# Staging VectorE and ScalarE work a step apart in a fused attention and two-MLP kernel

## The chip, the cores and the metric

The kernel runs on one core of a Trainium2 chip. The metric is device time in microseconds (us) of one execution: the median of several runs. TensorE (PE in the profile, its weight loads PEld) multiplies; VectorE (DVE) and ScalarE (ACT) do the elementwise work; SyncE (SP) starts nearly all DMAs. Each engine takes its instructions strictly in the order in which the program lists them for it.

## The reference

```python
# attention, per batch of 2:  S = 3008 tokens, 256 features, z has 64
scores = (1/S) * z @ z.T
x = u * (np.maximum(scores, 0)**2 @ v)          # 6016 x 256 over both batches
# first MLP, d_ff = 2048, scalars s and b
h = x @ w_in;  r = np.maximum(h, 0);  x = (s * (r*r) + b) @ w_out
# second MLP
h = x @ w_in2; x = (h / (1 + np.exp(-1.702*h))) @ w_out2
```

All inputs and the output are fp32.

## The kernel before

Every fp32 operand is split into a high part (a ScalarE copy that rounds to the matmul's type) and a low part (a VectorE subtract), and a product is three matmuls: high by high, high by low, low by high. The work is one list of 672 steps, built in advance:

- **Attention**, steps 0 to 287. A `Fresh` step makes a 128 x 512 block of scores; a `Turned` step uses the transpose of an earlier block, parked in HBM and fetched again (`park`, `fetch`). The second batch begins at step 144. `load_z` and `load_v` bring a column's inputs; `split_z` and `split_v` split them.
- **First MLP, plain part**, steps 288 to 319: two chunks of 512 tokens (m = 0 and 1), 16 `Mlp` steps each, one per slice of 128 of the 2048 hidden features. `up` is six matmuls into a PSUM bank, `between` is the elementwise work, `down` six matmuls into the two accumulators of the chunk. Beside it run `add_w` (adds the second weights over all 16 slices into `total`, from which `add_rows` gets the bias b times the sum, `shift`), and `sum_w` (sums of first weights that the later steps need).
- **First MLP, quads**, steps 320 to 479: five pairs of chunks (p = 1 to 5; the last pair has 448 tokens a chunk). A `Quad` does two slices for two chunks in four steps with seven products instead of eight, which costs extra adds on VectorE (`join`, line 691) and copies out of PSUM on ScalarE (`save`, line 681).
- **Second MLP**, steps 480 to 671: six pairs of the same kind, with the sigmoid gate.

The end of the kernel body is the order of everything. At position i of the main loop the program lists, in this order: step k = i + 5's `up` and `between`, what was put off until k (`due`, sorted by a rank), the side jobs planned for i (`todo`, filled by `when`), and then step i's `down`. So a step has five positions between its `up` and its `down`. Side jobs are the loads, the splits, the decoding of the weights (`decode_w`, five parts for each of 32 half-slices in each layer, on VectorE and ScalarE, whose result goes to HBM and comes back with `fetch_w`), and the preparation of the next pair (`gate`, `parts_of`, `split_part`). Below, a position is counted from the first `Mlp` step (288): "position 13" is i = 301.

Tiles come from small pools: five `w` tiles for raw, decoded and fetched weights, four `zu` tiles, 14 `big` tiles, four `a` and six each of `hi` and `lo` tiles, four PSUM banks `ps` and two pairs of accumulators.

When a chunk of the first MLP is done, `post` scales it and adds the bias: one ScalarE instruction for each of two halves (line 535), and stores the result to HBM.

Of the kernel before, what the change touches and what calls it, by code (L numbers as in the profile page):

```python
# [7 lines left out]
F32 = mybir.dt.float32  # L8
# [7 lines left out]
def attention_mlp_mlp_kernel(  # L16
# [24 lines left out]
    nc = tc.nc  # L41
# [32 lines left out]
    def ring_tile(name):  # L74
        return ring.tile([P, CH], F32R, tag="ring", name=name)
# [156 lines left out]
    def decode_w(layer, j, k, part):  # L232

        raw = staged["w", layer, j, k]
        low, high = raw[:, 0, :], raw[:, 1, :]
        if part == 0:
            pw = staged["pw", layer, j, k] = bits.tile([P, CH // 2], U32, tag="pw", name="pw")
            nc.vector.tensor_scalar(pw, high, 20, 0x7FF, ALU.logical_shift_right, ALU.bitwise_and)  # L240
        elif part == 1:
            pw = staged["pw", layer, j, k]
            nc.scalar.activation(out=pw, in_=pw, func=AF.Relu, scale=float(2**23), bias=rebias[:, 0:1])
            mt = staged["mt", layer, j, k] = bits.tile([P, CH // 2], U32, tag="mt", name="mt")
            nc.vector.tensor_scalar(mt, high, 0xFFFFF, 0x100000, ALU.bitwise_and, ALU.bitwise_or)
        elif part == 2:
            mt = staged["mt", layer, j, k]
            fr = staged["fr", layer, j, k] = bits.tile([P, CH // 2], F32, tag="fr", name="fr")
            nc.vector.scalar_tensor_tensor(fr, low, 2.0**-32, mt, ALU.mult, ALU.add)
        elif part == 3:  # L250
            pw = staged["pw", layer, j, k]
            nc.vector.scalar_tensor_tensor(pw, high, 0x80000000, pw, ALU.bitwise_and, ALU.bitwise_or)
        else:
            pw, fr = staged["pw", layer, j, k], staged["fr", layer, j, k]
            if k == 0:
                staged["wf", layer, j] = mid_tile(f"wf_{layer}_{j}")
            half = staged["wf", layer, j].rearrange("p (k n) -> p k n", k=2)[:, k, :]
            nc.vector.scalar_tensor_tensor(half, fr, 2.0**-20, pw.bitcast(F32), ALU.mult, ALU.mult)
            if k == 1:
                wf[layer, j] = hbm.tile([P, CH], F32, tag=f"wf_{layer}_{j}", name=f"wfh_{layer}_{j}")  # L260
                nc.sync.dma_start(out=wf[layer, j], in_=staged.pop(("wf", layer, j)))

    def fetch_w(layer, j):
        staged["wf", layer, j] = mid_tile(f"wb_{layer}_{j}")
        nc.sync.dma_start(out=staged["wf", layer, j], in_=wf[layer, j])

    def sum_w(layer, i):

        a1, a2 = [staged["wf", layer, 2 * i + n][:, : 2 * P].rearrange("p (k f) -> p k f", k=2) for n in range(2)]
        t = ew.tile([P, CH], F32, tag="a", name="ws", bufs=4)  # L270
        s1, s2, s3, s4 = [t[:, n * P : (n + 1) * P] for n in range(4)]
        nc.vector.tensor_tensor(out=s1, in0=a2[:, 0], in1=a2[:, 1], op=ALU.add)
        nc.vector.tensor_tensor(out=s2, in0=s1, in1=a1[:, 0], op=ALU.subtract)
        nc.vector.tensor_tensor(out=s3, in0=a1[:, 0], in1=a2[:, 0], op=ALU.subtract)
        nc.vector.tensor_tensor(out=s4, in0=a1[:, 1], in1=s2, op=ALU.subtract)
        both = sums[layer, i] = room[i // 2][:, i % 2]
        nc.scalar.copy(out=both[:, 0], in_=t)
        nc.vector.tensor_tensor(out=both[:, 1], in0=t, in1=both[:, 0], op=ALU.subtract)

    def add_w(j):  # L280

# [27 lines left out]
    def split_w(layer, j):  # L309
        src2 = staged["wf", layer, j].rearrange("p (k n) -> p k n", k=2)  # L310
        for k, ws in enumerate((wi, wo)):
            w = ring_tile(f"w_{layer}_{j}_{k}").rearrange("p (h n) -> p h n", h=2)
            nc.scalar.copy(out=w[:, 0, :], in_=src2[:, k, :])
            nc.vector.tensor_tensor(out=w[:, 1, :], in0=src2[:, k, :], in1=w[:, 0, :], op=ALU.subtract)
            ws[layer, j] = w
        wi[layer, j] = wi[layer, j].rearrange("p h (k f) -> p h k f", k=2)

# [151 lines left out]
    class Mlp:  # L469
# [15 lines left out]
                )  # L485

        def between(self):
            n = self.n
            a = ew.tile([P, CH], F32, tag="a", name="a", bufs=4)
            hi = self.hi = ew.tile([P, CH], F32R, tag="hi", name="hi", bufs=6)  # L490
            lo = self.lo = ew.tile([P, CH], F32R, tag="lo", name="lo", bufs=6)
            nc.scalar.activation(out=a[:, :n], in_=self.p[:, :n], func=AF.Relu)
            nc.scalar.activation(out=a[:, :n], in_=a[:, :n], func=AF.Square)
            nc.scalar.copy(out=hi[:, :n], in_=a[:, :n])
            nc.vector.tensor_tensor(out=lo[:, :n], in0=a[:, :n], in1=hi[:, :n], op=ALU.subtract)

        def down(self):
            j = self.j
            if j == 0:
                self.acc[:] = acc_pair(self.acc.pop(), "accm")  # L500
            add_hidden(self.layer, j, self.hi, self.lo, self.n, self.acc, j == 0, j == NF - 1)
            if j == NF - 1:
                for d in range(2):
                    post(self.layer, self.m, d, self.acc)

    def add_hidden(layer, j, hi, lo, n, acc, first, last, hold=False):
        w = wo[layer, j]
# [15 lines left out]
        for i, d in order:  # L523
            if hold and d == 1:
                held.append((add, i, d))
            else:
                add(i, d)

    def post(layer, m, h, acc):
        start, n = tokens(m)  # L530
        if layer == 0:
            if h == 0:
                staged["y"] = big_tile(f"y_{m}").rearrange("p (d n) -> p d n", d=2)
            y = staged["y"]
            nc.scalar.activation(
                out=y[:, h, :n], in_=acc[h][:, :n], func=AF.Identity, scale=sb[:, 0:1], bias=shift[:, h : h + 1]
            )
            if h == 1:
                store_rows(1, m, y)
            return  # L540
# [65 lines left out]
        )[k]  # L606
        nc.vector.tensor_tensor(out=x[to], in0=x[first], in1=x[second], op=ALU.subtract)

    def split_part(layer, p, k):
        n = tokens(2 * p)[1]  # L610
        src = staged["parts", layer, p][TERMS[k]]
        to = big_tile(f"op_{layer}_{p}_{k}", F32R).rearrange("p (h n) -> p h n", h=2)
        xs[layer, p, TERMS[k]] = to
        nc.scalar.copy(out=to[:, 0, :n], in_=src)
        nc.vector.tensor_tensor(out=to[:, 1, :n], in0=src, in1=to[:, 0, :n], op=ALU.subtract)

    banks = []

# [210 lines left out]
    for bb in range(B):  # L829
        for c in range(NCH):  # L830
            first = at["f", bb, 0, c, 0]
            v0 = min(at["f", bb, c, c, 0], at.get(("t", bb, 0, c, 0), len(steps)))
            if (bb, c) == (0, 0):
                sz = -20
                when(-40, load_z, bb, c)
                when(-18, load_v, bb, c)
            else:
                sz = first - LAG - 10 if (bb, c) != (0, 1) else -12
                ahead = 14 if (bb, c) in ((1, 0), (1, 1)) else 0
                when(max(sz - 8 - ahead, -39 if bb == 0 and c < 2 else -LAG), load_z, bb, c)  # L840
                when(max(v0 - LAG - 16 - ahead, -17), load_v, bb, c)
            for i in range(3):
# [14 lines left out]
    slots = ([turns[i * len(turns) // (10 * NF)] for i in range(10 * NF)], range(at["m", 1, 2], len(steps)))  # L857
    for layer in range(2):
        n = 0
        for j in range(NF):  # L860
            for k in range(2):
                when(slots[layer][n - 6] if n > 5 else slots[layer][0] - (4 if layer else 14) + n, load_w, layer, j, k)
                for part in range(5):
                    when(slots[layer][n], decode_w, layer, j, k, part)
                    n += 1
        for j in range(NF):
            if layer == 0:
                free = [2 + 5 * (i + 1) for i in range(LASTC)]
                i = next((i for i in range(LASTC) if 2 * j + 2 <= free[i]), LASTC)
                p = ends[i] + 2 * (j - (free[i - 1] // 2 if i else 0))  # L870
            else:
                p = at["q", 0, NP - 1, j // 2] + 4 + 2 * (j % 2)
                if j % 2:
                    when(p + 1, sum_w, layer, j // 2)
            when(p - (5 if layer else 8), fetch_w, layer, j)
            when(p, split_w, layer, j)
    start = at["m", 0, 0]
    for n, i in enumerate((0, 1, 2, 3, 6, 7, 4, 5)):
        use = start + 4 + 3 * n // 2
        for j in (2 * i, 2 * i + 1):  # L880
            when(use - 2, fetch_w, 0, j)
            when(use, add_w, j)
        if i < 6:
            when(use, sum_w, 0, i)
        else:
            for j in (2 * i, 2 * i + 1):
                when(start + 21 + i, fetch_w, 0, j)
            when(start + 23 + i, sum_w, 0, i)
    when(start + 15, add_rows)
    for i in (0, 0, 12, 28):  # L890
        when(start + i, settle)
    for m in range(2):
# [6 lines left out]
    for layer in range(2):  # L899
        for p in range(1 - layer, NP):  # L900
            first = at["q", layer, p, 0] - LAG
            for x in range(4):
# [79 lines left out]
```

## Time and profile before

| | |
|---|---|
| Median of 3 runs | 1492.48 us (1492.07 to 1494.46) |
| Profiled execution: its time, and its span from first to last instruction | 1493.18 us, 1491.3 us |
| TensorE busy | 1446.3 us, 97% of the span |
| VectorE busy | 1163.5 us, 78% |
| ScalarE busy | 1117.8 us, 75% |
| Mean granted TensorE clock | 0.991 |

The profile is of one execution. Busy time of the TensorE includes matmuls that ran at a lower clock. Idle time of an engine matters only where it ends up on the path that sets the end.

### The profile page before, as it was taken

How to read it: one execution, taken by the hardware profiler on the slowest of the kernel's cores; microseconds unless marked ns; L12 is line 12 of the kernel's file. 1: busy time of each engine (PE TensorE's matmuls, PEld its weight loads, DVE VectorE, ACT ScalarE, POOL GpSimd, SP SyncE). 2: the span in 40 equal slices, each digit the busy share in tenths (PEclk: the TensorE clock that was granted, in tenths of full speed). 3: DMA queues.
4: the chain of work that ended last, by engine and by line, in shares of the span. 5: the costliest groups of instructions: out<-in, count | busy, mean ns of one | idle time of the engine just before them, and what ended most of it. 6: DMA issues, size and time to landing. Idle time of an engine off the chain costs nothing.

```text
span 1491.3 us, 19079 instructions
## 1 busy us (share of the span) xinstructions
PE 1446.3 (97%) x6404; PEld 1201.4 (81%) x6404; DVE 1163.5 (78%) x2202; ACT 1117.8 (75%) x2068; POOL 0.3 (0%) x6
## 2 busy tenths in 40 slices
PE   8999999999999779999999999999999999999998
PEld 6888888888888667888878788877888888888896
DVE  7898988898897745877777676888878787787875
ACT  8888777988797666788878787886756666666664
POOL 0000000000000000000000000000000000000000
PEclk9999999999999989999999999999999999999999
DMA  5686784776795713213141312220020202020001
GB/s 130 180 213 192 213 226 106 186 214 187 196 233 128 236 43 101 62 44 91 37 106 43 99 43 92 74 73 27 1 57 1 57 1 57 1 45 9 16 14 25
DMA packets 191458, 143.86 MB, mean 96 GB/s; under 512 B 131712, under 2 KB 155776, under 8 KB 188800
## 3 DMA queue, kind: packets, MB, share of 16 engines
q1 hardware_dynamic: 188160, 142.03, 36.1%
q8 instruction: 50, 0.82, 0.2%
q10 hardware_dynamic: 3200, 0.62, 0.2%
q14 instruction: 48, 0.39, 0.1%
HBM read 87.69 MB, written 54.92 MB: 96 GB/s over the span
## 4 chain that ended last, share of the span: by engine, by line
PE 83%; ACT 7%; DVE 6%; DMA 1%; issue 1%; SPq 0%; ACTq 0%; DVEq 0%
PE accq L515 28%; PE ps_d L636 7%; PE ps_b L636 7%; PE ps_c L636 7%; PE acc L325 4%; PE acc L324 4%; PE acc L329 4%; PE tac L324 3%; PE tac L325 3%; PE ps_a L636 3%; PE tac L329 3%; PE ps_h L483 2%; PE ps_s L347 2%; PE ps_s L348 2%; PE accm L515 2%; DVE lo L730 1%
## 5 line engine op out<-in xcount | busy, mean ns | idle before, releaser
L515 PE MATMUL accq<-hi,w 128*128 128x512 f32 (+1 forms) x1408 | 375.0, 385 | 0.1
L729 ACT CAST hi<-a 128x512 fp32r<-128x512 f32 (+1 forms) x352 | 210.6, 609 | 181.5 <-DVE a L718 133.7
L515 PEld LDWEIGHTS accq<-hi,w 128*128 128x128 f32 x1408 | 264.2, 188 | 49.9 <-ACT hi L729 0.7
L730 DVE TENSOR_TENSOR lo<-a,hi 128x512 fp32r<-128x512 f32 (+1 forms) x352 | 233.1, 675 | 63.5 <-ACT hi L729 56.6
L515 PE MATMUL accq<-lo,w 128*128 128x512 f32 (+1 forms) x704 | 218.0, 385 | 0.0
L515 PEld LDWEIGHTS accq<-lo,w 128*128 128x128 f32 x704 | 132.2, 188 | 25.4 <-DVE lo L730 0.7
L325 PE MATMUL acc<-hi,v 128*128 128x512 f32 (+1 forms) x336 | 128.9, 384 | 2.0 <-DVE v L190 2.0
L324 PE MATMUL acc<-hi,v 128*128 128x512 f32 (+1 forms) x336 | 128.6, 383 | 0.2 <-ACT v L189 0.2
L718 DVE TENSOR_TENSOR a<-a,wg 128x512 f32<-128x512 f32 (+1 forms) x144 | 97.2, 675 | 29.8 <-ACT wg L707 29.7
L365 DVE TENSOR_TENSOR lo<-a,hi 128x512 fp32r<-128x512 f32 (+1 forms) x166 | 109.5, 660 | 3.7
L354 ACT ACTIVATE a<-a 128x512 f32<-128x512 f32 (+1 forms) x168 | 103.7, 617 | 5.5
L379 DVE STREAM_TRANSPOSE T<-a 128x512 f32<-128x512 f32 (+1 forms) x120 | 79.8, 665 | 31.7 <-ACT a L354 28.9
L353 ACT ACTIVATE a<-ps_s 128x512 f32<-128x512 f32 (+1 forms) x168 | 96.6, 575 | 8.8 <-PE ps_s L348 8.5
L329 PE MATMUL acc<-lo,v 128*128 128x512 f32 (+1 forms) x332 | 100.0, 382 | 0.0
L324 PE MATMUL tac<-hi,v 128*128 128x512 f32 x240 | 94.5, 394 | 3.4 <-DVE x L467 3.4
L325 PE MATMUL tac<-hi,v 128*128 128x512 f32 x240 | 94.1, 392 | 0.0
L707 ACT ACTIVATE wg<-a 128x512 f32<-128x512 f32 (+1 forms) x144 | 86.3, 622 | 0.0
L447 DVE TENSOR_TENSOR lo<-R,hi 128x512 fp32r<-128x512 f32 x110 | 74.2, 685 | 5.9 <-ACT hi L444 5.7
L721 ACT ACTIVATE a<-a 128x512 f32<-128x512 f32 (+1 forms) x120 | 74.6, 622 | 3.2
L444 ACT CAST hi<-R 128x512 fp32r<-128x512 f32 x120 | 68.0, 617 | 11.7 <-PE acc L325 3.0
L362 ACT CAST hi<-a 128x512 fp32r<-128x512 f32 (+1 forms) x120 | 72.4, 603 | 3.9
L325 PEld LDWEIGHTS acc<-hi,v 128*128 128x128 f32 x336 | 63.1, 188 | 14.5 <-DVE v L190 3.6
(130 smaller groups left out, 2750.8 us busy)
## 6 DMA issues: line engine op xcount, KB each, us to landing
R<-H SPq DMA_DIRECT2D x100, 256.0 KB, 6.0
H<-T SPq DMA_DIRECT2D x20, 1024.0 KB, 4.9
wb<-wfh SPq DMA_DIRECT2D x52, 256.0 KB, 3.4
wr<-in_moe_w_in_dram SPq DMA_DIRECT2D x32, 256.0 KB, 3.6
wr<-in_moe_w_out_dram SPq DMA_DIRECT2D x32, 256.0 KB, 3.1
wfh<-wf SPq DMA_DIRECT2D x32, 256.0 KB, 2.1
f<-rows SPq DMA_DIRECT2D x16, 512.0 KB, 4.3
H<-T SPq DMA_DIRECT2D x10, 512.0 KB, 3.2
```

What stands on the lines that cost most here:

```text
L324: nc.tensor.matmul(acc[d][:, :n], w[:, 0, cols], hi, start=first, stop=False)
L325: nc.tensor.matmul(acc[d][:, :n], w[:, 1, cols], hi, start=False, stop=last and not whole)
L329: nc.tensor.matmul(acc[d][:, :n], w[:, 0, cols], lo, start=False, stop=last)
L353: nc.scalar.activation(out=a[:, :n], in_=self.p[:, :n], func=AF.Relu, scale=1.0 / S)
L354: nc.scalar.activation(out=a[:, :n], in_=a[:, :n], func=AF.Square)
L365: nc.vector.tensor_tensor(out=lo[:, :n], in0=a[:, :n], in1=hi[:, :n], op=ALU.subtract)
L515: nc.tensor.matmul(acc[d][:, :n], w[:, h, d * P : (d + 1) * P], g[:, :n], start=first and i == 0, stop=last and i == 2,)
L636: nc.tensor.matmul(bank[:, :n], a[h], x[:, g, :n], start=first and j == 0, stop=last and j == 2, skip_group_check=True,)
L707: nc.scalar.activation(out=g[:, :n], in_=v[:, :n], func=AF.Sigmoid, scale=1.702)
L718: nc.vector.tensor_tensor(out=t[:, :n], in0=v[:, :n], in1=self.g[:, :n], op=ALU.mult)
L729: nc.scalar.copy(out=hi[:, :n], in_=v[:, :n])
L730: nc.vector.tensor_tensor(out=lo[:, :n], in0=v[:, :n], in1=hi[:, :n], op=ALU.subtract)
```

## The change

Six things are done.

1. In `Mlp`, `between` no longer issues its four instructions at once: Relu and Square (`act`) come at step k, after what else is due at k, and the copy and the subtract (`split`) at step k + 1.
2. `sum_w`, `split_part` and, in the second MLP, `split_w` are cut into parts that are issued one position apart: VectorE's first work, ScalarE's copy, VectorE's subtract.
3. The eight rounds of `add_w`, each with two fetched slices, move from positions 4, 5, 7, 8, 10, 11, 13, 14 to 4, 7, 10, 13, 16, 18, 20, 23; `add_rows` moves from 15 to 25, and the `post` of the first chunk (`end_chunk`) from 15 to 27, inside the second chunk.
4. `post` of the first MLP is a VectorE instruction instead of a ScalarE one.
5. The decoding of the second MLP's weights takes 140 positions instead of 160, and their `fetch_w`, `sum_w` and `split_w` in the last pair are issued in a new order, the sum ahead of the splits. The first layer's store of a decoded slice is issued three positions later.
6. `load_z` and `load_v` of the second batch's first two columns are issued 16 positions earlier, `parts_of` and `split_part` one earlier.

```diff
-                wf[layer, j] = hbm.tile([P, CH], F32, tag=f"wf_{layer}_{j}", name=f"wfh_{layer}_{j}")
-                nc.sync.dma_start(out=wf[layer, j], in_=staged.pop(("wf", layer, j)))
+                staged["done", layer, j] = staged.pop(("wf", layer, j))
+    def store_w(layer, j):
+        wf[layer, j] = hbm.tile([P, CH], F32, tag=f"wf_{layer}_{j}", name=f"wfh_{layer}_{j}")
+        nc.sync.dma_start(out=wf[layer, j], in_=staged.pop(("done", layer, j)))
...
-    def sum_w(layer, i):
+    def sum_w(layer, i, part):
+        if part:
+            t, both = staged["ws", layer, i], sums[layer, i]
+            if part == 1:
+                nc.scalar.copy(out=both[:, 0], in_=t)
+            else:
+                nc.vector.tensor_tensor(out=both[:, 1], in0=t, in1=both[:, 0], op=ALU.subtract)
+            return
...
-        both = sums[layer, i] = room[i // 2][:, i % 2]
-        nc.scalar.copy(out=both[:, 0], in_=t)
-        nc.vector.tensor_tensor(out=both[:, 1], in0=t, in1=both[:, 0], op=ALU.subtract)
+        sums[layer, i] = room[i // 2][:, i % 2]
...
         def between(self):
+            k = at["m", self.m, self.j]
+            later(k, 30, self.act)
+            later(k + 1, 10, self.split)
+        def act(self):
             n = self.n
-            a = ew.tile([P, CH], F32, tag="a", name="a", bufs=4)
+            a = self.a = ew.tile([P, CH], F32, tag="a", name="a", bufs=4)
+            nc.scalar.activation(out=a[:, :n], in_=self.p[:, :n], func=AF.Relu)
+            nc.scalar.activation(out=a[:, :n], in_=a[:, :n], func=AF.Square)
+        def split(self):
+            n, a = self.n, self.a
             hi = self.hi = ew.tile([P, CH], F32R, tag="hi", name="hi", bufs=6)
             lo = self.lo = ew.tile([P, CH], F32R, tag="lo", name="lo", bufs=6)
-            nc.scalar.activation(out=a[:, :n], in_=self.p[:, :n], func=AF.Relu)
-            nc.scalar.activation(out=a[:, :n], in_=a[:, :n], func=AF.Square)
             nc.scalar.copy(out=hi[:, :n], in_=a[:, :n])
             nc.vector.tensor_tensor(out=lo[:, :n], in0=a[:, :n], in1=hi[:, :n], op=ALU.subtract)
...
-            if j == NF - 1:
-                for d in range(2):
-                    post(self.layer, self.m, d, self.acc)
+            if j == NF - 1 and self.m:
+                end_chunk(self.m, self.acc)
...
+    def end_chunk(m, acc):
+        for d in range(2):
+            post(0, m, d, acc)
...
-            nc.scalar.activation(
-                out=y[:, h, :n], in_=acc[h][:, :n], func=AF.Identity, scale=sb[:, 0:1], bias=shift[:, h : h + 1]
-            )
+            nc.vector.tensor_scalar(y[:, h, :n], acc[h][:, :n], sb[:, 0:1], shift[:, h : h + 1], ALU.mult, ALU.add)
...
-                ahead = 14 if (bb, c) in ((1, 0), (1, 1)) else 0
+                ahead = 30 if (bb, c) in ((1, 0), (1, 1)) else 0
...
-    slots = (..., range(at["m", 1, 2], len(steps)))
+    slots = (..., [at["m", 1, 2] + n * 7 // 8 for n in range(10 * NF)])
...
+            when(slots[layer][n - 1] + 3 - 3 * layer, store_w, layer, j)
...
-                p = at["q", 0, NP - 1, j // 2] + 4 + 2 * (j % 2)
-                if j % 2:
-                    when(p + 1, sum_w, layer, j // 2)
-            when(p - (5 if layer else 8), fetch_w, layer, j)
-            when(p, split_w, layer, j)
+                p = at["q", 0, NP - 1, j // 2] + 4 - j % 2
+                for x in range(3 * (j % 2)):
+                    when(p - 3 + x, sum_w, layer, j // 2, x)
+            when(p - (7 - j % 2 if layer else 8), fetch_w, layer, j)
+            when(p, split_w, layer, j, 0)
+            when(p + layer, split_w, layer, j, 1)
...
-    for n, i in enumerate((0, 1, 2, 3, 6, 7, 4, 5)):
-        use = start + 4 + 3 * n // 2
+    for i, use in zip((0, 1, 2, 3, 6, 7, 4, 5), (4, 7, 10, 13, 16, 18, 20, 23)):
         for j in (2 * i, 2 * i + 1):
-            when(use - 2, fetch_w, 0, j)
-            when(use, add_w, j)
...
+            when(start + use - 2, fetch_w, 0, j)
+            when(start + use, add_w, j)
...
+        for x in range(3):
+            when(start + (use if i < 6 else 17 + 2 * i) + x, sum_w, 0, i, x)
-    when(start + 15, add_rows)
+    when(start + 25, add_rows)
+    when(start + 27, end_chunk, 0, steps[start].acc)
...
-                when(first - 15 + x, parts_of, layer, p, x)
+                when(first - 16 + x, parts_of, layer, p, x)
             for k in range(len(TERMS)):
-                when(first - 11 + k if k < 5 else first - 13 + 2 * k, split_part, layer, p, k)
+                for x in range(2):
+                    when(x + (first - 12 + k if k < 5 else first - 13 + 2 * k), split_part, layer, p, k, x)
```

## Rows read from the trace of the kernel before

**Rows 1.** The page, busy time of the engines.
```profile
PE 1446.3 (97%) x6404; PEld 1201.4 (81%) x6404; DVE 1163.5 (78%) x2202; ACT 1117.8 (75%) x2068; POOL 0.3 (0%) x6
```

**Rows 2.** Stretches: length; busy (x count) PE, PEld, DVE, ACT, POOL; PEclk, DMA share, GB/s.
```profile
180.00:200.00 20.00, 20.00 (x97) 17.78 (x96) 18.69 (x49) 18.22 (x37) 0.00 (x0) 1.00 0.68 189
200.00:220.00 20.00, 16.86 (x73) 14.45 (x72) 14.60 (x37) 12.30 (x24) 0.00 (x0) 0.91 1.04 239
...
500.00:520.00 20.00, 11.88 (x45) 9.14 (x45) 14.62 (x33) 12.30 (x22) 0.00 (x0) 0.83 0.74 251
520.00:540.00 20.00, 12.54 (x54) 10.19 (x53) 12.31 (x29) 9.92 (x17) 0.00 (x0) 0.84 0.15 49
...
580.00:600.00 20.00, 17.83 (x77) 14.08 (x76) 13.81 (x31) 13.79 (x25) 0.00 (x0) 1.00 0.60 153
...
660.00:680.00 20.00, 19.16 (x84) 15.21 (x83) 10.53 (x21) 15.67 (x29) 0.00 (x0) 1.00 0.58 153
```

**Rows 3.** Waits of TensorE, whole run: us in total, times, longest.
```profile
PE ps_d L636 <- ACT s L681: 10.5, 15, 2.1
PE ps_h L483 <- DVE Rx L571: 8.1, 2, 6.9
PE ps_t L296 <- DVE wt L292: 7.5, 1, 7.5
```

**Rows 4.** Chain that ended last, 470 to 570 us: start, us, what.
```profile
478.21 1.36 PE ps_h L483 x6
...
480.94 1.36 PE ps_h L483 x6
...
489.10 1.38 PE ps_h L483 x6
...
553.84 1.36 PE ps_h L483 x6
```

**Rows 5.** Timeline around 510 us: start, us, engine, line, [idle before].
```profile
508.42 0.59 ACT L492 ACTIVATE a<-ps_h 128x512 f32<-128x512 f32 x1
...
509.04 0.63 ACT L493 ACTIVATE a<-a 128x512 f32<-128x512 f32 x1
...
509.71 0.62 ACT L494 CAST hi<-a 128x512 fp32r<-128x512 f32 x1
510.36 0.69 DVE L495 TENSOR_TENSOR lo<-a,hi 128x512 fp32r<-128x512 f32 x1 [1.03 <-ACT hi L494]
510.96 0.88 DVE L286 TENSOR_TENSOR zeros<-zeros,wb 128x256 f32<-128x256 f32 x2
...
512.81 0.62 ACT L277 CAST Ts<-ws 128x512 fp32r<-128x512 f32 x1 [2.49 <-DVE ws L275]
...
513.33 0.59 ACT L492 ACTIVATE a<-ps_h 128x512 f32<-128x512 f32 x1
```

**Rows 6.** Stretches as before: 16 MLP steps, and around the last pair.
```profile
489.10:553.84 64.74, 49.16 (x197) 39.62 (x197) 39.16 (x86) 37.57 (x65) 0.00 (x0) 0.87 0.46 152
...
900.00:1020.00 120.00, 110.19 (x506) 93.13 (x505) 92.42 (x205) 97.87 (x205) 0.00 (x0) 1.00 0.26 83
```

**Rows 7.** Groups by line, 470 to 570 us: the last two of `add_rows`.
```profile
L292 DVE TENSOR_TENSOR wt<-zeros,wt 128x256 fp32r<-128x256 f32 x1 | 0.4, 417 | 0.0
L291 ACT CAST wt<-zeros 128x256 fp32r<-128x256 f32 x1 | 0.4, 399 | 0.0
```

**Rows 8.** Timeline at the second batch's beginning.
```profile
208.78 0.29 DVE L240 TENSOR_SCALAR pw<-wr 128x256 uint32<-128x256 uint32 x1 [3.55 <-DMA wr<-in_moe_w_in_dram]
...
209.82 0.76 PE L324 MATMUL tac<-hi,v 128*128 128x512 f32 x1 [3.14 <-DVE x L467]
```

**Rows 9.** Chain that ended last, 195 to 222 us.
```profile
213.27 0.23 PE tac L324
```

**Rows 10.** Instructions that read an accumulator: ns minimum/median/maximum.
```profile
L535 ACT ACTIVATE y<-accq,shift,sb x20: 715/767/781, 665.5 to 1006.7; 128x512 f32<-128x512 f32 x16, 128x448 f32<-128x448 f32 x4
...
L467 DVE TENSOR_TENSOR x<-tac,x x60: 679/683/687, 54.4 to 480.5; 128x512 f32<-128x512 f32 x60
```

More of the change, by code (lines that the diff above doesn't have):

```diff
@@ L265, in fetch_w @@
         nc.sync.dma_start(out=staged["wf", layer, j], in_=wf[layer, j])
-    def sum_w(layer, i):
+    def sum_w(layer, i, part):
[6 more added lines that the diff above has]
+            return
         a1, a2 = [staged["wf", layer, 2 * i + n][:, : 2 * P].rearrange("p (k f) -> p k f", k=2) for n in range(2)]
-        t = ew.tile([P, CH], F32, tag="a", name="ws", bufs=4)
+        t = staged["ws", layer, i] = ew.tile([P, CH], F32, tag="a", name="ws", bufs=4)
         s1, s2, s3, s4 = [t[:, n * P : (n + 1) * P] for n in range(4)]
@@ L307, in settle, with split_w @@
         room.append(wide_tile(f"{'RTTR'[n]}s_{n}", F32R).rearrange("p (i h n) -> p i h n", i=2, h=2))
-    def split_w(layer, j):
+    def split_w(layer, j, part):
         src2 = staged["wf", layer, j].rearrange("p (k n) -> p k n", k=2)
         for k, ws in enumerate((wi, wo)):
[L312 to L316, printed above, removed]
+            if part == 0:
+                w = staged["w", j, k] = ring_tile(f"w_{layer}_{j}_{k}").rearrange("p (h n) -> p h n", h=2)
+                nc.scalar.copy(out=w[:, 0, :], in_=src2[:, k, :])
+            else:
+                w = staged["w", j, k]
+                nc.vector.tensor_tensor(out=w[:, 1, :], in0=src2[:, k, :], in1=w[:, 0, :], op=ALU.subtract)
+                ws[layer, j] = w if k else w.rearrange("p h (k f) -> p h k f", k=2)
     def add_up(acc, w, hi, lo, n, first, last, whole):
@@ L607, in parts_of, with split_part @@
         nc.vector.tensor_tensor(out=x[to], in0=x[first], in1=x[second], op=ALU.subtract)
-    def split_part(layer, p, k):
+    def split_part(layer, p, k, part):
         n = tokens(2 * p)[1]
         src = staged["parts", layer, p][TERMS[k]]
+        if part:
+            to = xs[layer, p, TERMS[k]]
+            nc.vector.tensor_tensor(out=to[:, 1, :n], in0=src, in1=to[:, 0, :n], op=ALU.subtract)
+            return
         to = big_tile(f"op_{layer}_{p}_{k}", F32R).rearrange("p (h n) -> p h n", h=2)
@@ L614, in split_part @@
         nc.scalar.copy(out=to[:, 0, :n], in_=src)
-        nc.vector.tensor_tensor(out=to[:, 1, :n], in0=src, in1=to[:, 0, :n], op=ALU.subtract)
     banks = []
@@ L856, in attention_mlp_mlp_kernel @@
     turns = [i for i in range(16, ends[0] - 12) if i not in busy]
-    slots = ([turns[i * len(turns) // (10 * NF)] for i in range(10 * NF)], range(at["m", 1, 2], len(steps)))
+    slots = ([turns[i * len(turns) // (10 * NF)] for i in range(10 * NF)], [at["m", 1, 2] + n * 7 // 8 for n in range(10 * NF)])
     for layer in range(2):
@@ L871, in attention_mlp_mlp_kernel @@
             else:
-                p = at["q", 0, NP - 1, j // 2] + 4 + 2 * (j % 2)
-                if j % 2:
-                    when(p + 1, sum_w, layer, j // 2)
-            when(p - (5 if layer else 8), fetch_w, layer, j)
-            when(p, split_w, layer, j)
+                p = at["q", 0, NP - 1, j // 2] + 4 - j % 2
[4 more added lines that the diff above has]
+            when(p + layer, split_w, layer, j, 1)
     start = at["m", 0, 0]
-    for n, i in enumerate((0, 1, 2, 3, 6, 7, 4, 5)):
-        use = start + 4 + 3 * n // 2
+    for i, use in zip((0, 1, 2, 3, 6, 7, 4, 5), (4, 7, 10, 13, 16, 18, 20, 23)):
         for j in (2 * i, 2 * i + 1):
-            when(use - 2, fetch_w, 0, j)
-            when(use, add_w, j)
[L883 to L888, printed above, removed]
-    when(start + 15, add_rows)
+            when(start + use - 2, fetch_w, 0, j)
+            when(start + use, add_w, j)
+            if i > 5:
+                when(start + 15 + 2 * i, fetch_w, 0, j)
+        for x in range(3):
+            when(start + (use if i < 6 else 17 + 2 * i) + x, sum_w, 0, i, x)
+    when(start + 25, add_rows)
+    when(start + 27, end_chunk, 0, steps[start].acc)
     for i in (0, 0, 12, 28):
```

## The prediction

> **What bounds the kernel now.** I read the page first, then the run in stretches of 20 us, then the waits of TensorE, then the timeline in the stretches with gaps. TensorE is busy for 1446.3 of 1491.3 us [rows 1], so only the 45 us in which it is idle, and the matmuls that ran at a lower clock, can be won without taking work from it, and the change takes none. The stretches show where that is. About 11 us lie at the two ends of the run, which the change does not touch. The rest sits in five places [rows 2]: at 200 to 220 us (the second batch begins, clock 0.91), at 500 to 540 (the plain part of the first MLP, clock 0.83 and 0.84), at 580 to 600 (its end), at 660 to 680 (the first change of pair; two more like it lose 0.85 and 0.68), and around the last pair of the first MLP, 900 to 1020, where 9.8 of 120 us are idle [rows 6]. The waits name the releasers: the copies out of PSUM on ScalarE, the split of the second chunk, and `add_rows` [rows 3]. After 1020 the second MLP runs without gaps worth naming. None of the three engines is full over the run; what costs is order, within these places.
>
> **The first MLP's plain part.** An undisturbed `Mlp` step lasts 2.73 us, from one `up` to the next. From the `up` at 489.10 to the one sixteen steps later, at 553.84, 64.74 us pass [rows 4]; sixteen steps are 43.7, so 21.1 us are lost here. That is the 15.6 us of idle time at 500 to 540 [rows 2] and some 5.5 of matmuls at the lower clock behind them.
>
> The timeline shows how it comes about [rows 5]. In a step with a `sum_w`, ScalarE does Relu, Square and the high part (508.42 to 510.33), VectorE then the low part, two `add_w` and four small sums, and only then can ScalarE copy the sum (512.81, after an idle time of 2.49); its next Relu stands behind that copy, at 513.33. So each engine waits for the other once a step and the round takes 4.91 us against TensorE's 2.73. Six such rounds, with `gate` and `add_w` in between, use up the five positions between `up` and `down`. What is late then is the split of the second chunk (TensorE waits 6.9 us for it) and `add_rows` (7.5 us) [rows 3].
>
> The change cuts the round at both ends. VectorE's subtract comes after a copy that waits for a Square of the step before, and ScalarE's copy of a sum comes one position after the four sums, so neither is asked for something just begun. The sums are also spread: the six come at positions 4, 7, 10, 13, 20 and 23 instead of 4, 5, 7, 8, 13 and 14. In these sixteen steps VectorE is now busy 39.2 us and ScalarE 37.6 [rows 6], 90% and 86% of the undisturbed 43.7. Counting positions 4 to 19 in both versions, VectorE loses two sums (the four small ones take from 511.84 to 512.8, 0.95, and a subtract like the low part's 0.69), four `add_w` (0.44 each) [rows 5] and `add_rows` (0.42 [rows 7] and two short ones), and gains a few tenths: 5.6 us less, so 77%. ScalarE loses two copies (0.62 each), two `post` (0.77 each [rows 10]) and a copy, and gains 0.6: 2.6 us less, so 80%. What went out comes back at positions 20 to 25, where VectorE then has 14.4 us of work in six steps of 16.4. The most VectorE falls behind in any step, adding up its instructions step by step, is 1.3 us; its low part is wanted four steps (10.9 us) after the `up`. I therefore take the stalls as gone, the one for the split of the second chunk included: its copy and subtract end some 2.6 us after the `up` of their position and TensorE wants them 4.1 after it.
>
> One wait stays. `add_rows` puts four matmuls into TensorE's list right behind an `up`, and they need a ScalarE copy that stands behind Relu and Square of that same `up`: 0.59 + 0.63 [rows 5] + 0.40 + 0.42 [rows 7] = 2.04 us, 2.1 with the hand-overs, and 0.4 for the matmuls (an estimate). It was there before, inside the 7.5. Below it can't go. Above, 3.14 us of idle time at 206 to 209 brought the clock down [rows 8], a gap of 2.1 did not [rows 3, 6]; this one is nearer to the latter, and if the clock fell it would cost 1.6 more. I take 2.5: 18.6 of 21.1 come back.
>
> The extra step of delay for each high and low part costs nothing, since the 10.9 us cover it; without that cover it would be up to 2.73 us a step. Behind VectorE's subtract, which can wait for a copy, stand `add_w` and `gate`, which have two positions of slack.
>
> **The end of the plain part.** At 580 to 600 2.2 us are idle [rows 2], ScalarE again waiting for sums before a copy that frees a bank. The sums are staged now, but VectorE gets the first chunk's `post`, the second's, two sums and the decoding within positions 25 to 33, by my count 21.6 us of work in nine steps of 24.5. I take back 1.7.
>
> **`post` on VectorE.** ScalarE needs 767 ns for one. VectorE's nearest instruction, an add from an accumulator, takes 683 [rows 10]; I take 0.68, between 0.2 less and 0.1 more. VectorE is half idle at the changes of pair (10.5 us busy in 660 to 680, ScalarE 15.7 [rows 2]). Where `post` waits for TensorE's last matmul, the low part of a quad stands behind it on VectorE, where before ScalarE's copies out of PSUM stood; the `join` that frees a bank is due a step later and has 2.7 us to spare. The three gaps of 0.84, 0.85 and 0.68 shrink: 1.6 of 2.4.
>
> One rule speaks against this move. The Trainium skill (Perfetto Trace Analysis, Optimizing Scalar/DVE Operations) puts the overhead of an access to PSUM at about 125 ns for VectorE and 51 for ScalarE. By that the 24 instructions would be some 1.8 us dearer in all; measured, VectorE's read of an accumulator is the shorter one [rows 10], and the sum goes by that.
>
> **The last pair.** Its steps are shorter (448 tokens) while the side work is not: the end of the decoding, all splits and sums of the next weights. The gaps are ScalarE's copies out of PSUM, late because ScalarE waited for sums [rows 3]. VectorE is busy for 92.4 and ScalarE for 97.9 of 110.2 undisturbed us [rows 6], 84% and 89%. The change takes eight `post` (5.9) and four or five decoding parts (256 wide, 0.40 as in [rows 7]: 1.8) from ScalarE, which comes to 82%; VectorE gains the `post` (5.4), loses some 17 decoding parts (0.29 [rows 8] to 0.42 [rows 7]: 6.1) and stays at 83%. The sums are staged as above. But for two quads, where `split_part` comes on top, ScalarE has about 11 us of work in 9.7, and ScalarE still waits for VectorE's part of c22. Between 0.5 and all 9.8 us could stay; I take 3.5, near the sums: 6.3 back. Decoding faster puts one part more on each seven positions earlier, 0.05 us a step on a VectorE that is busy for 10.5 to 14 of 20 us there [rows 2]: nothing while it has that room, and 0.05 a step, 6 us over 120, without it.
>
> **The second batch.** At 205.04 the raw weights of one slice are asked for, and VectorE waits 3.55 us for them [rows 8]; behind it stands the add that frees an accumulator, and TensorE waits 3.14. The next eight matmuls take until 213.27 [rows 9], 3.45 us where eight at 0.23 are 1.84: together 4.7 us. In SP's list the weights stand behind four DMAs each of `load_z` and `load_v`, while the DMA engines are full (share 1.04, 0.68 in the 20 us before [rows 2]). These eight go 16 positions forward, with eight of the next column; the store of a decoded slice, for which SP waits until VectorE has made it, goes three positions back. Each of these weights is asked for six positions before VectorE wants it, which eight more issues ahead of it do not use up. I take back 4.3, between 0 and 4.7.
>
> The Trainium skill (DMA: Bandwidth & Descriptors, Why small descriptors are slow) says that every packet has a fixed cost, worst for short ones, and `load_z` moves runs of 128 bytes. By that rule the earlier place fills up as the later one did; that is the third rival.
>
> **The sum.** 18.6 + 1.7 + 1.6 + 6.3 + 4.3 = 32.5 us, from the profiled execution's own 1493.18: 1460.7. The median of the runs is 0.7 below that execution, so 1460.0. All of it but the wait in `add_rows` would be 38.1: 1454.4.
>
> **Rivals and chances.**
> - *Forecast*, 0.63: 1454 to 1466.
> - *The last pair stays as it is*, 0.17: ScalarE keeps too much work there, or VectorE, with `post` on it, hands over c22 later. 1460.0 + 6.3 = 1466.3. For it: 11 us of work in 9.7. Against: the gaps follow the waits for sums.
> - *The batch's stall moves*, 0.08: the early loads fill the DMA engines around 165 to 185 us and another fetch comes late. 1464.3. Against: share 0.68 [rows 2].
> - *The stages do not part the engines*, 0.07: ScalarE still stands at the copy of a sum because VectorE runs later than a position behind; half of the plain part's gain (9.3) is not had: 1469.3, and 1470.9 if the clock falls again.
> - *Slower*, 0.03: the low part, issued a step later, is late at `down` in the plain part. It decides from 1.0 us a step on (32 steps eat the 32.5 us won); a whole step of 2.73 in each would cost 87 and give 1460 + 87 = 1547. Against: a plain round of 2.6 us in 13.6.
>
> That leaves 0.02 for no change. The range 1454 to 1472 holds the first three cases and most of the fourth, some 0.85. Faster by over 0.2% (3 us, about what a measurement of this kernel can tell from no change) 0.95, within it 0.02, slower 0.03.
>
> **What would show it.** In the plain part: no idle time of TensorE at 495 to 520 us, clock 1.0, the wait for `wt` at 2 to 2.5 us and some ten steps later than before, ScalarE's waits for `ws` gone. At the batch's beginning: full TensorE, weights landing before VectorE wants them. In the last pair: ScalarE's waits for `ws` gone and the waits of `ps_b` and `ps_d` cut by two thirds. Wrong would be a wait of `ps_d` or `ps_b` that stays, a first `down` waiting for `lo`, or VectorE at its limit behind a `post`.

## The result, and the profile after

| | before | after |
|---|---|---|
| Median | 1492.82 us (1492.07 to 1494.46, 4 runs) | 1455.95 us (1455.25 to 1458.7, 4 runs) |
| Profiled execution: time, span | 1493.18 us, 1491.3 us | 1458.7 us, 1456.9 us |
| Mean granted TensorE clock | 0.991 | 0.996 |

The ratio is 0.9755, with a 95% interval of 0.9738 to 0.9772: 36.9 us less, where 32.5 were forecast. The profiled execution of after is the slowest of its four; between the two profiled ones lie 34.5 us. All readings of places in this section are of these two.

The page's busy times answer to [rows 1]: TensorE has the same 6404 matmuls, is busy for 8.1 us less, and its idle time has gone from 45 to 18.7 us, some 11 of them at the two ends of the run as before.

```profile
PE 1438.2 (99%) x6404; PEld 1200.0 (82%) x6404; DVE 1179.6 (81%) x2226; ACT 1100.0 (75%) x2044; POOL 0.3 (0%) x6
```

The run in stretches, with the columns of [rows 2]. The places that had gaps are full, except three: 200 to 240, 540 to 560, and a remnant in the last pair.

```profile
200.00:220.00 20.00, 19.26 (x92) 16.65 (x91) 18.13 (x44) 16.34 (x32) 0.00 (x0) 1.00 0.88 240
220.00:240.00 20.00, 18.87 (x86) 15.72 (x85) 16.32 (x32) 12.96 (x26) 0.00 (x0) 1.00 0.71 140
500.00:520.00 20.00, 20.00 (x90) 16.55 (x89) 16.23 (x33) 15.58 (x27) 0.00 (x0) 1.00 0.55 195
520.00:540.00 20.00, 20.00 (x90) 16.55 (x89) 14.41 (x33) 15.95 (x29) 0.00 (x0) 1.00 0.26 79
540.00:560.00 20.00, 17.36 (x65) 13.93 (x64) 10.24 (x24) 10.32 (x21) 0.00 (x0) 0.83 0.19 65
580.00:600.00 20.00, 20.00 (x90) 16.56 (x89) 17.38 (x32) 15.24 (x28) 0.00 (x0) 1.00 0.17 32
660.00:680.00 20.00, 20.00 (x90) 16.57 (x89) 16.84 (x32) 15.16 (x29) 0.00 (x0) 1.00 0.21 54
880.00:1000.00 120.00, 117.21 (x547) 101.25 (x546) 100.24 (x205) 95.10 (x201) 0.00 (x0) 1.00 0.23 72
```

The waits of TensorE answer to [rows 3]. The wait for the split of the second chunk (`Rx`, 8.1 us) is gone, that for `add_rows` (`wt`) is 2.6 instead of 7.5, and `ps_d` 1.2 instead of 10.5.

```profile
PE ps_t L304 <- DVE wt L300: 2.6, 1, 2.6
PE tac L334 <- DVE x L477: 2.1, 3, 1.1
PE acc L335 <- DVE v L190: 2.0, 4, 0.7
PE ps_b L658 <- ACT s L703: 1.6, 3, 0.9
PE ps_d L658 <- ACT s L703: 1.2, 2, 0.9
```

The chain that ended last, from 470 us, answers to [rows 4]. From 489.13 to 540.81 each `up` comes 2.72 us after the one before. Then 10.50 us pass for two steps (5.44): 5.06 lost at `add_rows`, and the `up` at 551.31 itself took 2.56 us instead of 1.36.

```profile
489.13 1.36 PE ps_h L493 x6
...
532.65 1.36 PE ps_h L493 x6
...
540.81 1.38 PE ps_h L493 x6
...
547.53 1.06 PE ps_t L304 x4
...
551.31 2.56 PE ps_h L493 x6
```

Where the time came from is read by setting the same matmul, by its number in TensorE's order, side by side in both traces; the difference grows where time is won. In us:

| place | forecast | won |
|---|---|---|
| beginning of the second batch | 4.3 | 2.7 (3.8 won at first, 1.1 given back at 230 us) |
| plain part and its end | 18.6 + 1.7 | 17.6 (6.5 lost again at `add_rows`, so 24.1 elsewhere) |
| three changes of pair | 1.6 | 3.8 (1.24, 1.29, 1.31) |
| last pair | 6.3 | 9.3 |
| the rest, mostly the end of the run | 0 | 0.9 |

Each figure compares one execution with one. Set beside after in the same way, the eleven runs below that keep the early loads take from 1.4 us less to 0.5 more for the matmuls from 150 to 480 us, with the same code there; so the 2.7 stands for something between 2.1 and 4.1. The 0.9 is not the change's: runs 2 and 3, with the code of after there, lose the same 1.2 us at the end of the run as the kernel before.

### The profile page after: what moved, and what is told of

Its sections match the earlier page's. It is cut to its first block, busy times and chain, and to the rows that moved or that the text cites. A ratio compares the mean times of both kernels' runs of the same rounds, so it can differ in the third digit from the quotient of the medians.

```text
span 1456.9 us, 19100 instructions
## 1 busy us (share of the span) xinstructions
PE 1438.2 (99%) x6404; PEld 1200.0 (82%) x6404; DVE 1179.6 (81%) x2226; ACT 1100.0 (75%) x2044; POOL 0.3 (0%) x6
## 4 chain that ended last, share of the span: by engine, by line
PE 87%; ACT 6%; DVE 3%; DMA 2%; issue 1%; SPq 1%; ACTq 0%; DVEq 0%
PE accq L532 29%; PE ps_d L658 8%; PE ps_c L658 7%; PE ps_b L658 7%; PE acc L335 4%; PE acc L334 4%; PE acc L339 4%; PE ps_a L658 4%; PE tac L334 3%; PE tac L335 3%; PE tac L339 3%; PE accm L532 3%; PE ps_h L493 3%; PE ps_s L357 2%; PE ps_s L358 2%; DMA R<-H 1%
## 5 line engine op out<-in xcount | busy, mean ns | idle before, releaser
L713 DVE TENSOR_TENSOR a<-ps_c,s 128x512 f32<-128x512 f32 (+1 forms) x88 | 59.5, 676 | 22.0 <-PE ps_c L658 21.8
L454 ACT CAST hi<-R 128x512 fp32r<-128x512 f32 x120 | 67.8, 617 | 12.1 <-DMA R<-H 6.0
```

## The experiments

All start from the changed kernel. Ratios are to the kernel before on the same chip, whose medians there were 1495.06 (runs 1 to 4), 1493.36 (the four runs without a number) and 1493.43 us (runs 5 to 8). Between these groups, and with after, ratios are compared and not medians.

### What removed the stalls of the plain part

The prediction named three means at once: `Mlp` staged, sums staged, sums spread. Two theories stood against each other, that the staging carries the gain because it cuts the round between the engines, and that the spreading does because it takes work out of the positions. Undoing the one that carries it should bring back the wait for the second chunk's split. The fourth run goes after what was left, the wait of `add_rows`.

Run 1, `Mlp` at once:

```diff
-            later(k, 30, self.act)
-            later(k + 1, 10, self.split)
+            self.act()
+            self.split()
```

> The changed kernel, but the four elementwise instructions of an Mlp step are issued at once again, as before the change; everything else stays. Theory A (the plain part was slow because two engines had too much work in ten positions, and spreading the sums is what mends it): 0 to 3 us slower than the changed kernel's 1456, TensorE without gaps there but for add_rows. Theory B (the two engines took turns inside a step, and staging is what mends it): 8 to 17 us slower, with waits for the split of the second chunk back.

Run 2, the plain part's sums at once:

```diff
-            when(start + (use if i < 6 else 17 + 2 * i) + x, sum_w, 0, i, x)
+            when(start + (use if i < 6 else 17 + 2 * i), sum_w, 0, i, x)
```

> The changed kernel, but the three parts of each sum_w of the first MLP are issued at one position; places of the sums and the Mlp stages stay. Theory A (spreading): 0 to 3 us slower than 1456; ScalarE waits 1 to 1.5 us for each of eight sums, which two free positions in three absorb. Theory B (staging): 8 to 17 us slower.

Run 3, the sums at their old positions:

```diff
-    for i, use in zip((0, 1, 2, 3, 6, 7, 4, 5), (4, 7, 10, 13, 16, 18, 20, 23)):
+    for i, use in zip((0, 1, 2, 3, 6, 7, 4, 5), (4, 5, 7, 8, 10, 11, 13, 14)):
```

> The changed kernel with all its stages, but the rounds of add_w and sum_w are at positions 4, 5, 7, 8, 10, 11, 13, 14 again (add_rows and the first chunk's post stay late). Theory A (spreading): VectorE runs some 5 us late around position 10 and the split of the second chunk is late by 2 to 6 us: 1458 to 1464, TensorE waiting for Rx. Theory B (staging): 0 to 2 us slower than 1456, no such wait.

None of the three brought the stall back. Both theories fell: undoing any one costs between nothing and about 2 us by the ratios. So a third was formed (C below), that any one of the three takes enough off; against it stood a fourth (D), that the later place of `add_rows` had done it alone. They were tested by undoing all three and by leaving one at a time.

> The changed kernel with all three means for the plain part undone: Mlp steps at once, sums at once, old places of the sums; add_rows and the first chunk's post stay late and the rest of the change stays. Theory C (any one of the three takes enough of the load off; undoing one alone cost 0 to 2 us): the stall for the split of the second chunk is back, 7 to 12 us before 520 us, 1466 to 1472 in all. Theory D (what cost was above all add_rows in the first half of the second chunk, whose move alone mends it): below 1461, TensorE's wait for Rx under 3 us.

> Of the three means only the new places of the sums: Mlp steps and sums at once. Theory C: within 4 us of the changed kernel's 1456, TensorE without a wait for Rx, or one under 2 us. Theory D: the same. If two means are needed: 1462 or more.

> Of the three means only the staged sums: Mlp steps at once, old places. VectorE has 5 us more to do by position 10 than in the changed kernel. Theory C: wait for Rx 1 to 4 us, 1457 to 1461. If two means are needed: the wait is above 5 us, 1462 or more.

> Of the three means only the staged Mlp steps: sums at once, old places. ScalarE stands at each sum's copy until VectorE has made it, in consecutive positions. Theory C: wait for Rx 1 to 4 us, 1457 to 1461. If two means are needed: above 5 us, 1462 or more.

| kept of the three | median, us | ratio (95%) | wait for `Rx` | wait for `wt` |
|---|---|---|---|---|
| all (after) | 1455.95 | 0.9755 (0.9738 to 0.9772) | none | 2.6 |
| sums staged, spread (run 1) | 1460.77 | 0.9768 (0.9754 to 0.9783) | none | 4.7 |
| `Mlp` staged, spread (run 2) | 1458.07 | 0.9755 (0.9736 to 0.9774) | 1.4 | 2.1 |
| `Mlp` and sums staged (run 3) | 1458.31 | 0.9752 (0.9737 to 0.9767) | 1.4 | 2.1 |
| spread only | 1466.54 | 0.9823 (0.9803 to 0.9844) | 2.7 | 8.0 |
| sums staged only | 1460.37 | 0.9782 (0.9761 to 0.9803) | 2.4 | 3.9 |
| `Mlp` staged only | 1463.38 | 0.9802 (0.9782 to 0.9822) | 5.1 | 2.1 |
| none | 1470.34 | 0.9845 (0.9829 to 0.9862) | 8.1 | 4.2 |

With none, the old wait is back to the tenth of a microsecond, and the stretch in which it lies reads like the one in [rows 2]. That refutes the fourth theory. By matmul order 12.1 of the 17.6 us are given back; 5.5 stay won, 2.7 of them at the end of the plain part and the rest at `add_rows`, which costs 7.9 us there and 11.0 before. Its later place was kept in every run. Its waits of TensorE, and in a second block the stretch:

```profile
PE ps_h L493 <- DVE Rx L589: 8.1, 2, 6.9
PE ps_t L304 <- DVE wt L300: 4.2, 1, 4.2
```

```profile
500.00:520.00 20.00, 11.90 (x43) 9.16 (x42) 15.16 (x32) 11.50 (x20) 0.00 (x0) 0.74 0.71 247
```

The third theory holds for one of the three only: with the sums staged alone the wait and the median came as it said. With `Mlp` staged alone they came as forecast for the case that two means are needed (5.1 us, 1463.38), and spreading alone moves the congestion on to `add_rows` and is the slowest. What is left is weaker: any two suffice, one does not. The order of the three is not firm, as they had two executions each and the interval of `Mlp` staged only overlaps both others. Waits of TensorE with spreading only, and in a second block the stretch of `add_rows`:

```profile
PE ps_t L304 <- DVE wt L300: 8.0, 1, 8.0
PE ps_h L493 <- DVE Rx L589: 2.7, 1, 2.7
```

```profile
540.00:560.00 20.00, 12.04 (x46) 9.68 (x45) 10.22 (x24) 11.06 (x20) 0.00 (x0) 0.76 0.25 82
```

### The wait that stayed

Run 4 stages `add_rows` like the rest: ScalarE's copy at position 24, VectorE's subtract at 25, the four matmuls and the bias at 26.

```diff
-    def add_rows():
+    def add_rows(part):
...
+        if part == 0:
+            nc.scalar.copy(out=hi, in_=total)
+            return
+        if part == 1:
+            nc.vector.tensor_tensor(out=lo, in0=total, in1=hi, op=ALU.subtract)
+            return
...
-    when(start + 25, add_rows)
+    for x in range(3):
+        when(start + 24 + x, add_rows, x)
```

> The changed kernel, but add_rows is staged too: ScalarE's copy at position 24, VectorE's subtract at 25, the four matmuls and the bias at 26. The trace of the changed kernel shows TensorE waiting 2.64 us for it and some 20 matmuls at the lower clock behind that wait, 6.5 us together in that execution. If the wait is the cause of the lower clock: no gap at 540 to 550 us, clock 1.00, profiled execution near 1452, median 1452 to 1454. If the clock falls there for another reason, or VectorE is late anyway: gap smaller, clock still 0.83 in that stretch, 1454 to 1456.

Measured: 1454.08 us (1451.55 to 1455.31), ratio 0.9722 (0.9708 to 0.9737). The wait is 0.3 us, and the stretch is full:

```profile
540.00:560.00 20.00, 19.67 (x89) 16.06 (x88) 13.78 (x31) 13.03 (x25) 0.00 (x0) 1.00 0.42 131
```

Against the trace of after, 5.4 us are won exactly there. It is the fastest version of the study; its interval ends at 0.9737, where that of the changed kernel begins at 0.9738.

How large the wait is, and what it costs, is read from the timeline of after at that place (start, us, engine, line, [idle before]):

```profile
543.36 1.52 PE L493 MATMUL ps_h<-Rx,w 128*128 128x512 f32 x6
...
544.92 0.60 ACT L505 ACTIVATE a<-ps_h 128x512 f32<-128x512 f32 x1
...
545.55 0.63 ACT L506 ACTIVATE a<-a 128x512 f32<-128x512 f32 x1
...
546.09 0.39 ACT L299 CAST wt<-zeros 128x256 fp32r<-128x256 f32 x1
...
546.45 0.69 DVE L277 TENSOR_TENSOR Ts<-ws,Ts 128x512 fp32r<-128x512 f32 x1
...
547.05 0.42 DVE L300 TENSOR_TENSOR wt<-zeros,wt 128x256 fp32r<-128x256 f32 x1
...
547.53 1.06 PE L304 MATMUL ps_t<-ones,wt 128*128 128x64 f32 x4 [2.64 <-DVE wt L300]
548.40 2.05 PE L532 MATMUL accm<-hi,w 128*128 128x512 f32 x4
```

ScalarE's three instructions follow the `up` without a break, as forecast. What was not forecast is VectorE's: the last part of a staged sum (`Ts`, for position 23 + 2 = 25) stands ahead of the subtract that TensorE waits for, and holds it up for 0.5 us. In run 3 the sums are elsewhere; its timeline at the same place, and in a second block the stretch:

```profile
546.52 0.39 ACT L299 CAST wt<-zeros 128x256 fp32r<-128x256 f32 x1
546.94 0.43 DVE L300 TENSOR_TENSOR wt<-zeros,wt 128x256 fp32r<-128x256 f32 x1 [0.49 <-ACT wt L299]
...
547.42 0.64 PE L304 MATMUL ps_t<-ones,wt 128*128 128x64 f32 x4 [2.10 <-DVE wt L300]
```

```profile
540.00:560.00 20.00, 17.90 (x81) 14.58 (x80) 10.06 (x24) 12.48 (x23) 0.00 (x0) 1.00 0.26 92
```

In run 3, as in run 2, the gap is 2.10 us, the clock stays at 1.00, and two steps take 2.85 us too long (the `up`s at 541.23 and 549.52 are 8.29 apart). In after the gap is 2.64 and the clock falls: 5.06 too long, and 1.4 more behind it, 6.5 in all. The four runs of the next part, which have the same gap of 2.6, show 0.91 in this stretch, where after shows 0.83; by matmul order the place costs them 4.9 to 5.0 us. And `Mlp` staged only has a gap of 2.10 there like runs 2 and 3, but its clock falls and it loses 4.5. So the longer gap is VectorE's doing; that it decided the fall of the clock is not shown (last section).

### `post`, the loads, and the last pair

Run 5, `post` back on ScalarE:

```diff
-            nc.vector.tensor_scalar(y[:, h, :n], acc[h][:, :n], sb[:, 0:1], shift[:, h : h + 1], ALU.mult, ALU.add)
+            nc.scalar.activation(
+                out=y[:, h, :n], in_=acc[h][:, :n], func=AF.Identity, scale=sb[:, 0:1], bias=shift[:, h : h + 1]
+            )
```

> The changed kernel with post of the first MLP on ScalarE again (the first chunk's still late). If post is what the gaps at the changes of pair were, about 1 us at each of four changes comes back, 3.8 us, and up to 3 us more around the last pair, where ScalarE then has 5.9 us more work: 1460 to 1463. If the staged split_part mended those gaps: 1456 to 1457, no TensorE wait for ScalarE's copies out of PSUM at the changes.

1463.18 us, 0.9799 (0.9781 to 0.9816). The same matmuls at the three changes of pair now come as in before: all 3.8 us are given back there, and 1.9 in the last pair. The waits of TensorE show the releaser, ScalarE's copies out of PSUM behind a `post`:

```profile
PE ps_d L660 <- ACT s L705: 4.5, 11, 0.6
```

Run 6, the second batch's first loads 16 positions later, as before (the later store is kept):

```diff
-                ahead = 30 if (bb, c) in ((1, 0), (1, 1)) else 0
+                ahead = 14 if (bb, c) in ((1, 0), (1, 1)) else 0
```

> The changed kernel with load_z and load_v of the second batch's first columns at their old, 16 positions later places. If the earlier loads freed the queue for the weights: 2.5 to 4 us slower than 1456 and a wait of TensorE of 2 to 3 us near 207 us. If the later store of the decoded slice (SP no longer waits for VectorE in front of the loads) did it: 1456 to 1457.

1461.4 us, 0.9786 (0.977 to 0.9801). The first gap is back (3.8 us) and the second, at 230 us, gone. The longest wait, and in a second block the two stretches:

```profile
PE tac L334 <- DVE x L477: 3.9, 2, 3.8
```

```profile
200.00:220.00 20.00, 16.24 (x69) 13.83 (x69) 14.50 (x36) 12.77 (x25) 0.00 (x0) 0.91 1.01 234
220.00:240.00 20.00, 20.00 (x95) 17.37 (x94) 17.36 (x33) 13.66 (x27) 0.00 (x0) 1.00 0.91 217
```

By matmul order the early loads win 4.5 us and lose 1.8 later, a net of 2.7; by the ratios it is 4.6 us, with intervals that just overlap. Behind this place the run is within 0.1 us of the kernel before, so the later store, which it keeps, shows no gain by itself.

Run 7, the last pair with the decoding over 160 positions and the old order of fetches, sums and splits, all at once (`post` stays on VectorE). Run 8, the old order alone, with the decoding over 140 positions:

```diff
-    slots = (..., [at["m", 1, 2] + n * 7 // 8 for n in range(10 * NF)])
+    slots = (..., range(at["m", 1, 2], len(steps)))
...
-                p = at["q", 0, NP - 1, j // 2] + 4 - j % 2
+                p = at["q", 0, NP - 1, j // 2] + 4 + 2 * (j % 2)
                 for x in range(3 * (j % 2)):
-                    when(p - 3 + x, sum_w, layer, j // 2, x)
-            when(p - (7 - j % 2 if layer else 8), fetch_w, layer, j)
+                    when(p + 1, sum_w, layer, j // 2, x)
+            when(p - (5 if layer else 8), fetch_w, layer, j)
             when(p, split_w, layer, j, 0)
-            when(p + layer, split_w, layer, j, 1)
+            when(p, split_w, layer, j, 1)
```

> The changed kernel, but the second MLP's weights are decoded over 160 positions and fetched, split and summed in the old order and all at once; post stays on VectorE and split_part staged. If decoding and order are what emptied the last pair's gaps: 6 to 9 us slower than 1456, ScalarE's waits for ws back. If it was post leaving ScalarE: under 3 us slower.

> As the run before, but with the faster decoding kept (140 positions): only the order and the stages of the last pair's sums and splits are undone. If the stages are what counts: nearly all of the previous run's loss, 5 to 8 us over 1456. If it is the decoding that left the pair: 0 to 3 us.

Run 7: 1465.22 us, 0.9809 (0.9793 to 0.9824). Run 8: 1460.27 us, 0.9776 (0.9760 to 0.9791). The stretch around the last pair, run 7 and then run 8:

```profile
880.00:1000.00 120.00, 112.72 (x516) 94.94 (x515) 100.32 (x215) 92.95 (x196) 0.00 (x0) 1.00 0.26 83
```

```profile
880.00:1000.00 120.00, 114.85 (x531) 98.12 (x530) 97.46 (x200) 94.09 (x197) 0.00 (x0) 1.00 0.21 72
```

By matmul order run 7 gives back about 7.0 us and run 8 about 3.5. So of the 9.3 won in the last pair some 3.5 come from decoding that is over before it, 3.5 from the order with its stages, and 1.9 from `post` (run 5). The old decoding under the new order was not tried, so how the two would add up the other way round stays open; as does which half of the new order, sum first or parts apart, does the work.

## Why the prediction was right, and where not

**Right: what bounds it.** Five places with idle time were named, the gain came from these, and TensorE's own work did not change.

**The plain part: the mechanism holds, but not all of it was needed.** The `up` at 489.10 before is the one at 486.41 here. The sixteen steps from it take 43.52 us, all of them with TensorE busy at clock 1.00. In them VectorE is busy for 33.60 and ScalarE for 34.79 us, 77% and 80%, as worked out.

```profile
486.41:529.93 43.52, 43.52 (x193) 36.04 (x193) 33.60 (x72) 34.79 (x62) 0.00 (x0) 1.00 0.58 188
```

What the prediction did not ask is whether the cuts and the spreading are each needed: any two leave at most 1.4 us of the wait for the split. The rival that the stages do not part the engines did not come.

**The term that was mis-sized: `add_rows`.** 2.5 us were left for it ("this one is nearer to the latter"), 6.5 it cost in the profiled execution. The chain on ScalarE was right (2.04 us; 2.10 of gap in runs 2 and 3, and 2.85 lost: 0.75 beyond the gap, where 0.4 was taken). Two things were not. VectorE's queue was not walked at that position, where the change itself had put a sum's last part; that is 0.54 us more of gap. And the clock then fell. The comparison of gaps that spoke against this (3.14 us brought it down, 2.1 did not) was too thin: with `Mlp` staged only it fell behind a gap of 2.10. The price of 1.6 for a fall was right: in runs 5, 6 and 8, with the gap of after, 5.0 less 2.64 and 0.75 leaves 1.6. In the profiled execution of after it was 3.1, 1.5 us more than in those three runs with the same code there. Without the 4.0 us over the term the plain part would have given 21.6, 1.3 more than the 20.3 forecast.

**The end of the plain part: the gain came, but not by the means named.** 2.8 us were won where 1.7 were taken. The prediction counted on the staged sums. With the sums at once, in run 2 and with none of the three, only 0.1 us is given back in this stretch; with `post` on ScalarE in run 5, nothing. Which of the other moves ended that wait stays open.

**The changes of pair: too small a term.** 1.6 of the 2.4 idle us were taken; 3.8 came back. Each place lost about 1.3 us though only 0.68 to 0.85 of it were idle, since the busy time of the matmuls around a gap was longer too. Run 5 shows `post` as the whole cause. What the argument said of durations was wrong: VectorE's `post`, by line over the run, takes 804 ns where 683 were assumed and ScalarE needed 767.

```profile
L556 DVE TENSOR_SCALAR y<-accq,sb,shift x20: 735/804/811, 645.3 to 974.8; 128x512 f32<-128x512 f32 x16, 128x448 f32<-128x448 f32 x4
```

The rule of the Trainium skill that was weighed against the move (Perfetto Trace Analysis, Optimizing Scalar/DVE Operations: some 125 ns of overhead for VectorE's access to PSUM, 51 for ScalarE's) had the direction right: 37 ns dearer, 0.9 us over 24 instructions where the rule gives 1.8 as an estimate. It decided nothing, because VectorE had room there and ScalarE's copies out of PSUM were what TensorE waited for.

**The last pair: too cautious.** (One point of the opening is wrong and bears on its side work: the weights are not fp32 but 64-bit floats, 256 KB for 128 x 256 values, and `decode_w` turns them into fp32.) 6.3 were taken back of 9.8 idle us; 9.3 came, matmuls that run faster without the gaps included, and 2.8 us are still idle from 880 to 1000. ScalarE's waits for the small sums, 7.0 us there before, are gone, and `ps_b` and `ps_d` together wait 2.8 instead of 14.2 us over the run: cut by four fifths, where two thirds were said.

**The second batch: the rival was half right.** 2.7 of 4.3. The stall of 3.14 us went, and a smaller one came at 230 us, which the kernel with late loads does not have. In the timeline of after, ScalarE waits for a parked block that is fetched back, and the add that frees an accumulator comes late behind it:

```profile
227.75 0.62 ACT L454 CAST hi<-R 128x512 fp32r<-128x512 f32 x1 [2.19 <-DMA R<-H]
...
230.65 0.47 PE L334 MATMUL tac<-hi,v 128*128 128x512 f32 x1 [1.13 <-DVE x L477]
```

That is the third rival's mechanism, another fetch late, some 50 us later than it was looked for; it gave back 1.1 of the 3.8 us won before it, 1.8 of 4.5 against run 6. How far 2.7 is from the 4.3 is not firm, as the same code came out up to 1.4 us better in other runs. The Trainium skill's rule on the fixed cost of packets (DMA: Bandwidth & Descriptors, Why small descriptors are slow) fits such a move; no run here separates packet cost from bytes or from the order of SP's list.

**The sum.** The profiled execution came 2.0 us below the 1460.7 of the sum: +3.0 (last pair), +2.2 (changes), +0.9 (rest), less 2.7 (plain part) and 1.6 (batch) make 1.8. That it came so near is partly luck: misses of 6.1 us on one side and 4.3 on the other nearly cancel, and the 0.9 is not the change's. The median lies another 2.75 below that execution, where 0.7 were taken. Whether the fall of the clock at `add_rows` is milder in the other executions, whose mean clock is 0.997 to 0.999 against 0.996, would fit but is not shown.

## What to carry to other kernels

When two in-order engines hand work to each other and back within a step, issue their two parts one step apart from each other, and then undo the measures one at a time, and all together: here any two of three did the work, and the wait that was left cost more than undoing any single one of them. A matmul that is put right behind the producer of its operands carries that whole chain as a gap; walk the queue of every engine on the chain at the very position where it is put, with what the change itself has moved there. An instruction may go to the engine on which it takes longer, if the other one stands between TensorE and its banks.

## What was not expected of the hardware

The length of a gap did not decide what it cost. At the same place TensorE was idle for 2.10 us in three runs. In runs 2 and 3 the granted clock stayed at 1.00 and 2.85 us were lost. With `Mlp` staged only it fell to 0.50, the lower of its two levels, and 4.5 were lost. The gap in that run's timeline, and in a second block a stretch behind it:

```profile
553.52 0.63 PE L304 MATMUL ps_t<-ones,wt 128*128 128x64 f32 x4 [2.10 <-DVE wt L300]
```

```profile
555.00:558.00 3.00, 3.00 (x8) 2.32 (x8) 0.94 (x3) 0.00 (x0) 0.00 (x0) 0.50 0.54 201
```

A gap of 2.64 us cost 5.0 in runs 5, 6 and 8 and 6.5 in after. Run 8's stretch at the place, and in a second block one of after behind the gap, where 16 matmuls take 6 us:

```profile
540.00:560.00 20.00, 17.36 (x72) 13.94 (x71) 11.12 (x27) 11.22 (x22) 0.00 (x0) 0.91 0.21 75
```

```profile
548.00:554.00 6.00, 6.00 (x16) 4.84 (x17) 1.75 (x5) 0.10 (x1) 0.00 (x0) 0.50 0.41 135
```

So the loss beyond the gap itself was 0.75 us without a fall, 2.4 with one in runs 5, 6 and 8 and with `Mlp` staged only, and 3.85 in after. What decides which of these a gap gets is not shown by these runs; without the gap (run 4) the clock stayed at 1.00.

In run 1's profiled execution the granted clock reads 0.95 nearly throughout, yet 90 matmuls pass in 20 us as at 1.00; there the reading did not show in the time.

```profile
520.00:540.00 20.00, 20.00 (x90) 16.58 (x89) 12.97 (x28) 16.85 (x29) 0.00 (x0) 0.95 0.24 76
```
